# A new order of opening, batches and end in a fused attention and expert kernel, with dummy products, two output transfers and one tiny product

## Chip, cores and metric

The kernel runs on one core of one Trainium2 chip. The metric is the time of one execution on the device in microseconds (us), which is the median over the runs shown. Engines are named as in the profile: PE is TensorE (matrix products), PEld its weight loads, DVE is VectorE, ACT is ScalarE, SP the engine whose queue issues nearly all transfers.

## What is computed

Eight batches of eight heads: 512 rows of `x` and 32 rows of `state`, 64 wide, attend to each other; the result goes through a two-layer network with the Mish activation, all in float32.

```python
scores = softmax(x @ state.T / 8);  xread = scores @ state        # [8, 8, 512, 64]
scores2 = softmax(state @ x.T / 8); sread = scores2 @ x           # [8, 8, 32, 64]
x = concat([xread, sread], axis=2) -> (8 * 544, 512)
h = x @ w_in                       # w_in  512 x 2048
g = h * tanh(log1p(exp(h)))        # Mish
out = g @ w_out                    # w_out 2048 x 512
```

## The kernel before

The read of the state is folded into the first layer: `a @ (state @ w_in)`, so a batch needs `sw = state @ w_in` (small products of tiles of 64 by 32, `sw_product`) and then 128 x 128 x 256 products of the attention weights with it (`gemm1`, letter P). A large product is done with two-part operands (a rounded high part and the rest), three products for one. The hidden width is worked through in 8 slots of 256 columns.

For batches 0 and 1 the second layer is plain (`gemm2_wide`, letter g, 12 products). From batch 2 on it is done by a seven-product scheme on halves (`sums`, `high`, `low`, then `gemm2`): step U issues 12 products into two accumulator banks, step V 9 into two others, and P issues 12. So one slot of a unit (half a batch) is 33 large products. After 8 slots `combine` adds the four banks into the output tile `o` and sends it. A last unit "s" does the rows of the state for all batches; its output goes out in eight transfers of 32 rows.

Order is written out by hand. Every engine but POOL issues strictly in the order of the program (class `InOrder`): `OPENING` lists steps up to the first slots of batch 2, and then a loop over `periods` runs P two slots ahead of U and V, with the side work of the next batch put at fixed slots by the tables `STEADY`, `LAST` and `END`. The letters that matter:

- `SC` scores of a batch (32 small products), `RE` the read of `x` (64), `SW`/`SX` the products `state @ w_in`: `SW_j` in the opening is 16 small products in batch 0 and 32 later, `SX_0` and `SX_4` are 64 each and cover slots 0 to 3 and 4 to 7 of the next batch. `sw_four` issues SX in two halves, into two kinds of PSUM bank; `xh`, `xl` are the two-part split of its result on ACT and DVE.
- `in_e` (`stream`) brings slot e of `w_in` back from DRAM (512 KB). There are four places only: slots 0, 1, 4, 5 share the tiles `wi6` and `wi7`, slots 2, 3, 6, 7 the tile `x`. So `in_4` to `in_7` can be issued only after SX_0 has read slots 0 to 3. `LX` (transposed `x` of a batch) uses `wi6` and `wi7` too, `LN` (`x` itself) uses the tile `x`.
- In the opening: `lx` loads the two halves of batch 0's transposed `x`, `li` and `Lo` the raw weights, `hi`, `ci`, `ji`, `ho`, `co`, `jo` turn them into float32 on ACT and DVE, `sca` to `pil` are batch 0's attention, `pq` its first-layer products, `fill` and `warm` products of the identity whose result nobody reads.

In every batch the loop runs, on PE, SX_0 after slot 11's first part, SX_4 after slot 14's, and in slot 2 of the next batch RE and, one part later, SC. Between SX_0 and SX_4 lie 99 large products, between SX_4 and RE 132, between RE and SC 9, and from SC to the next SX_0 288.

Of the kernel before, what the change touches and what calls it, by code (L numbers as in the profile page):

```python
# [63 lines left out]
def state_attention_mish_kernel(ctx, tc, xT, xn, st, wiw, wow, out):  # L64
# [705 lines left out]
    run(OPENING, a=0, b=1, c=2, d=3)  # L770

    for n, (u, s) in enumerate(periods):
        if n < SLOTS:
            continue
        b, h = u
        now = SLOTS * h + s
        table = END if b == "s" else LAST if b == B - 1 else STEADY
        extra = {k: [v] for k, v in table.get(now, {}).items()}

        def beside(place):  # L780
            who = {} if b == "s" else dict(a=b, b=b + 1, c=b + 2)
            for text in extra.get(place, ()):
                run(text, **who)

        one, two = n + 1 < len(periods), n + 2 < len(periods)
        if two:
            gemm1(n + 2)
        beside("a0")
        if one:
            high(n + 1)  # L790
        beside("v0")
        if one:
            low(n + 1)
        beside("a1")
        if two:
            mish(n + 2)
        gemm2(n, 0)
        beside("pe")
        gemm2(n, 1)
        beside("pe2")  # L800
        beside("v1")
        if two:
            sums(n + 2)
        beside("a2")
        if s == SLOTS - 1:
            combine(u)
        beside("v2")
# [3 lines left out]
    lb tab lx_0 sca_0 sma_0 sma_1 lx_1 li_0 fill_1 tur_0 sca_1 top_0 sma_2 li_1 sma_3 li_2 lev_0 tur_1 Lo_0  # L811
    top_1 ev_0 tot_0 gua_0 rec_0 ci_0 hi_0 lev_1 ev_1 hi_1 warm nor_0 bac_0 ji_0 a.SW_0 pih_0 tot_1 gua_1 pil_0
    rec_1 a.wh_0 a.wl_0 hi_2 nor_1 di_2 pq_0 Lo_1 bac_1 ci_1 ji_1 ho_0 a.SW_1 js_0 li_5 li_3 pih_1 co_0 pil_1
    fill_2 fill_2 ji_2 a.wh_1 mh_0 a.wl_1 jo_0 pq_1 mh_1 a.SW_2 ho_1 a.wh_2 wo_0 gi_1 ci_5 lo_0 gj_1 gi_0 a.wl_2
    p_1 hi_3 ci_3 gj_0 ma_1 do_1 mb_1 ji_3 gh_1 g_3 g_2 jo_1 Lo_6 g_1 g_0 gl_1 a.SW_3 a.wh_3 a.wl_3 p_2 b.LX
    Lo_2 ma_2 mb_2 wo_1 lo_1 Lo_4 ho_2 p_3 hi_5 Lo_3 co_3 li_4 hi_4 g_10 do_2 gh_2 jo_2 g_13 g_12 wo_2 lo_2 gl_2
    ci_4 ji_4 ho_4 g_11 ho_3 jo_3 wo_3 ji_5 g_20 Lo_5 ho_5 li_6 g_23 a.SW_4 a.wh_4 co_5 a.wl_4 lo_3 mb_3 g_22
    g_21 ma_3 a.SW_5 p_4 js_2 co_4 gh_3 gl_3 jo_4 b.LS hi_6 ci_6 a.t2 a.wh_5 ma_4 mb_4 gh_4 a.wl_5 g_32 li_7
    wo_4 g_30 g_33 ji_6 p_5 Lo_7 gl_4 lo_4 a.x2_1 a.SW_6 a.wh_6 a.wl_6 js_5 g_31 g_41 g_42 a.x2_0 jo_5 co_6 ho_6
    g_43 ma_5 mb_5 ci_7 a.TU wo_5 lo_5 js_3 a.s2 g_40 js_6 hi_7 b.SC p_6 b.sc_1 gh_5 gl_5 b.sc_0 ji_7 g_53  # L820
    a.SW_7 mb_6 ma_6 jo_6 wo_6 b.tu b.to a.wh_7 a.wl_7 gh_6 g_50 b.le g_51 ho_7 b.x1 lo_6 b.SW_0 gl_6 p_7 js_4
    g_52 g_61 ma_7 b.wh_0 mb_7 b.ts b.no js_1 b.ba g_60 co_7 a.BU b.ph_0 a.LN b.ph_1 b.wl_0 g_62 g_63 b.pl_0
    a.RE b.LN b.pl_1 p_8 gh_7 gl_7 a.ro js_7 jo_7 wo_7 ma_8 mb_8 b.SW_2 p_9 lo_7 g_70 g_71 g_72 b.wh_2 b.wl_2
    gh_8 gl_8 mb_9 g_73 o_0 ma_9 p_10 gh_9 gl_9 mb_10 b.t2 o_1 b.SW_6 ma_10 b.wh_6 p_11 g_83 g_93 gh_10 b.wl_6
    o_2 o_3 g_81 g_91 b.SW_4 gl_10 b.x2_1 g_80 b.x2_0 c.LX ma_11 b.TU qs_0 b.wh_4 b.wl_4 g_101 qs_1 c.LS c.SC
    g_82 kh_0 kl_0 mb_11 qh_0 gh_11 gl_11 g_92 p_12 c.sc_0 ql_0 d.LS g_90 in_1 c.sc_1 in_0 c.SW_0 mb_12 qs_6
    g_102 c.wh_0 c.tu g_103 c.to kh_1 ma_12 g_113 g_100 c.le g_110 c.x1 g_112 g_111 in_5 c.t2 gh_12 gl_12 c.x2_0
    b.s2 c.wl_0 qh_1 c.ts p_13 g_121 ql_1 ma_13 c.no kl_1 mb_13 gh_13 qs_7 g_122 c.x2_1 qh_7 p_14 b.BU b.RE in_4
    gl_13 g_123 qh_6 c.ba in_2 ql_6 c.ph_0 ql_7 c.pl_0 g_133 ma_14 g_131 g_132 g_120 mb_14 b.ro qs_4 qh_4 ql_4
    in_3 c.SW_2 gh_14 g_130 c.wh_2 gl_14 c.wl_2 p_15 g_140 qs_5 ma_15 P_0 qh_5 c.SW_4 g_141 qs_3 g_142 ql_5  # L830
    mb_15 gh_15 kh_3 gl_15 qh_3 g_150 g_143 c.TU M_0 g_151 S_0 in_6 c.wh_4 in_7 kl_3 H_0 o_4 ql_3 P_1 o_5 g_152
    g_153 c.wl_4 M_1 L_0 S_1 o_6 c.ph_1 H_1 L_1 o_7 P_2 U_0 V_0 P_3 M_2 d.LX kh_7 S_2 qs_2 V_1 P_4 H_2 kh_2 kl_2
    qh_2 L_2 kh_4 kl_4 ql_2 kl_7 M_3 c.pl_1 M_4 U_1 S_3 c.SW_6 c.BU c.wh_6 kh_5 c.wl_6 c.s2 U_2 P_5 H_3 V_2 L_3
    c.LN S_4 M_5 kl_5 S_5 H_4 L_4 d.SC P_6 V_3 V_4 kh_6 kl_6 U_3 in_0 d.sc_0 M_6 S_6 d.sc_1 c.RE H_5 U_4 d.tu
    c.ro H_6 d.to P_7 L_5 U_5 L_6 V_5 M_7 S_7 H_7 d.le P_8 M_8 L_7 V_6 U_6 S_8 H_8 d.t2 L_8 P_9 in_2 U_7 M_9 S_9
    V_7 in_3 C_0 in_1
# [3 lines left out]
STEADY = {  # L840
    2: dict(pe="a.RE", pe2="b.SC", v1="a.ro", a2="b.sc_0 b.sc_1", v2="in_0 in_1 in_2 in_3"),
    3: dict(v0="b.tu"),
    4: dict(v0="b.to"),
    5: dict(v0="b.le"),
    6: dict(v0="b.t2"),
    8: dict(a2="b.x1 b.x2_0 b.x2_1"),
    9: dict(v0="b.ts b.s2", v2="b.no"),
    10: dict(v2="b.ba"),
    11: dict(pe="b.SX_0", a2="b.xh_0", v2="b.xl_0 in_4 in_5 in_6 in_7"),
    12: dict(a2="b.ph_0 b.ph_1", v2="b.pl_0 b.pl_1"),  # L850
    13: dict(v2="b.TU b.BU"),
    14: dict(pe="b.SX_4", a2="b.xh_4", v2="b.xl_4 b.LN c.LX c.LS"),
}
LAST = {
    0: dict(v2="in_0 in_1"),
    2: dict(pe="a.RE", v1="a.ro", v2="in_2 in_3"),
    7: dict(pe="ST", a2="sh", v2="sl"),
    12: dict(a2="WH_0", v2="WL_0 in_4"),
    13: dict(a2="WH_1", v2="WL_1 in_5"),
    14: dict(a2="WH_2", v2="WL_2"),  # L860
    15: dict(a2="WH_3", v2="WL_3 in_6 in_7"),
}
END = {
    0: dict(a2="WH_4", v2="WL_4"),
    1: dict(a2="WH_5", v2="WL_5"),
    2: dict(a2="WH_6", v2="WL_6"),
    3: dict(a2="WH_7", v2="WL_7"),
}
# [28 lines left out]
```

## Time and profile before

| | us |
|---|---|
| median of three runs | 634.57 |
| lowest and highest run | 631.49, 635.59 |
| the profiled execution | 632.25 |
| its span, first to last instruction | 630.5 |
| busy in the span: PE / DVE / ACT | 609.2 / 478.3 / 339.3 |

The profile is of one execution. Matmuls overlap on PE, so a PE that is busy throughout can still run at different pitches; how far apart equal groups of products start tells the pitch. In the chain of work (the view that follows the last instruction back to what released it) a row gives start, length, engine, what is written and how many instructions.

### The profile page before, as it was taken

The page shows a single profiled execution, that of the slowest core. Times are in us where ns is not written, and L with a number is a line of the kernel's source. Part 1 is how long each engine was busy: PE and PEld are TensorE (multiplying, and loading weights), DVE is VectorE, ACT ScalarE, POOL GpSimd, SP SyncE. Part 2 cuts the span into 40 slices and gives each one's busy share as a digit, 9 for nine tenths or more (in the row PEclk, how much of TensorE's full clock was granted, in tenths as well). Part 3 has the DMA queues.
Part 4 walks back from the last instruction along what each step waited for, and adds up shares of the span by engine and source line. Part 5 has one row for each costly group of instructions (what it writes and reads, how often), then busy time and mean ns, then how long its engine had stood idle before and what let it go on. Part 6 is the DMA issues. An engine that isn't in the chain of part 4 may idle for free.

```text
span 630.5 us, 15205 instructions
## 1 busy us (share of the span) xinstructions
PE 609.2 (97%) x6548; PEld 582.9 (92%) x6548; DVE 478.3 (76%) x874; ACT 339.3 (54%) x497; POOL 0.7 (0%) x6
## 2 busy tenths in 40 slices
PE   4899999899999999999999999999999999999995
PEld 3798899899999999999999999999999999999995
DVE  4786896589788888588868797679858886577753
ACT  4988763456355564347634754456534663445541
POOL 0000000000000000000000000000000000000000
PEclk9899999999999999999999999999999999999998
DMA  8976443642175234601563047403551165101201
GB/s 334 411 306 269 126 150 111 171 165 68 20 217 199 68 131 145 200 40 45 158 210 134 35 137 233 142 35 114 164 191 45 40 169 202 61 35 68 102 1 33
DMA packets 57267, 86.43 MB, mean 137 GB/s; under 512 B 35825, under 2 KB 38897, under 8 KB 54001
## 3 DMA queue, kind: packets, MB, share of 16 engines
q1 hardware_dynamic: 57056, 85.34, 40.2%
q8 instruction: 51, 0.84, 0.5%
q14 instruction: 16, 0.12, 0.1%
q10 hardware_dynamic: 144, 0.13, 0.1%
HBM read 68.16 MB, written 17.30 MB: 136 GB/s over the span
## 4 chain that ended last, share of the span: by engine, by line
PE 90%; ACT 4%; DVE 2%; DMA 2%; issue 1%; SPq 1%; DVEq 0%; ACTq 0%
PE ph_u L56 25%; PE acc L56 11%; PE ph L56 6%; PE swp L56 4%; PE sc L56 2%; PE srp L56 1%; ACT L56 1%; PE acc_(5, 1)_2_5548 L56 1%; PE acc_(6, 1)_2_6474 L56 1%; PE acc_(4, 1)_2_4622 L56 1%; PE acc_(3, 1)_2_3696 L56 1%; PE acc_(2, 1)_2_2770 L56 1%; PE acc_(2, 0)_0_2269 L56 1%; PE acc_(6, 0)_2_6044 L56 1%; PE acc_(4, 0)_2_4192 L56 1%
## 5 line engine op out<-in xcount | busy, mean ns | idle before, releaser
L56 ACT CAST Sh<-G 128x896 fp32r<-128x896 f32 x104 | 98.2, 944 | 134.7 <-DVE G L56 48.7
L56 PE MATMUL ph_u<-aT,sw 128*128 128x256 f32 x1152 | 150.2, 280 | 0.0
L56 DVE TENSOR_TENSOR Sl<-G,Sh 128x896 fp32r<-128x896 f32 x104 | 112.9, 1086 | 44.7 <-ACT Sh L56 44.2
L56 PEld LDWEIGHTS ph_u<-aT,sw 128*128 128x128 f32 x1152 | 141.0, 189 | 2.1 <-issue 2.1
L56 DVE TENSOR_TENSOR G<-G 128x128 f32<-128x128 f32 (+1 forms) x312 | 104.7, 335 | 22.0 <-ACT G L56 14.2
L56 PE MATMUL acc<-wo,gh 128*128 128x256 f32 x512 | 90.1, 280 | 0.0
L56 ACT ACTIVATE G<-ph_u 128x512 f32<-128x512 f32 x104 | 62.2, 599 | 49.3 <-PE ph_u L56 45.9
L56 PEld LDWEIGHTS acc<-wo,gh 128*128 128x128 f32 x512 | 77.4, 188 | 3.4 <-issue 3.3
L56 PE MATMUL acc<-wo,gl 128*128 128x256 f32 x256 | 71.1, 278 | 0.0
L56 PEld LDWEIGHTS ph<-aT,sw 128*128 128x128 f32 x384 | 47.0, 193 | 8.4 <-ACT turned L56 5.0
L56 PE MATMUL ph<-aT,sw 128*128 128x256 f32 x384 | 50.3, 287 | 4.0 <-ACT turned L56 2.5
L56 ACT CAST sw<-swp 128x512 fp32r<-128x512 f32 (+1 forms) x72 | 34.3, 549 | 29.4 <-PE swp L56 29.4
L56 PEld LDWEIGHTS acc<-wo,gl 128*128 128x128 f32 x256 | 48.4, 189 | 0.0
L56 DVE TENSOR_TENSOR sw<-swp,sw 128x512 fp32r<-128x512 f32 (+1 forms) x72 | 41.0, 623 | 9.5 <-ACT sw L56 9.5
L56 ACT ACT_TABLE_LOAD x29 | 37.2, 1283 | 8.2 <-PE ph L56 5.7
L56 PE MATMUL swp<-wi,bd 64*32 64x256 f32 x1024 | 33.8, 381 | 0.6 <-DVE wi L56 0.5
L56 ACT ACTIVATE turned<-ph 128x512 f32<-128x512 f32 (+1 forms) x34 | 18.5, 574 | 20.8 <-PE ph L56 16.1
L56 DVE STREAM_TRANSPOSE e<-sc 128x512 f32<-128x512 f32 x30 | 19.5, 688 | 9.5 <-ACT sc L56 9.3
L56 PEld LDWEIGHTS swp<-wi,bd 64*32 64x32 f32 x1024 | 18.4, 106 | 7.1 <-PE at L56 1.0
L56 DVE CAST gh<-turned 128x1024 fp32r<-128x1024 f32 (+1 forms) x17 | 11.2, 660 | 16.3 <-ACT turned L56 9.2
L56 PE MATMUL ph_u<-srT,whl 128*128 128x256 f32 x192 | 23.1, 276 | 0.0
L56 PEld LDWEIGHTS ph_u<-srT,whl 128*128 128x128 f32 x192 | 22.4, 188 | 0.0
(446 smaller groups left out, 1205.4 us busy)
## 6 DMA issues: line engine op xcount, KB each, us to landing
wi<-w_dram SPq DMA_DIRECT2D x56, 512.0 KB, 5.0
wir<-in_wi_dram SPq DMA_DIRECT2D x8, 1024.0 KB, 9.3
wor<-in_wo_dram SPq DMA_DIRECT2D x8, 1024.0 KB, 12.4
xn<-in_xn_dram SPq DMA_DIRECT2D x8, 1024.0 KB, 6.5
out_dram<-o SPq DMA_DIRECT2D x32, 256.0 KB, 3.2
xT<-in_xT_dram SPq DMA_DIRECT2D x14, 512.0 KB, 7.8
w_dram<-wi SPq DMA_DIRECT2D x8, 512.0 KB, 6.2
e_dram<-e SPq DMA_DIRECT2D x32, 128.0 KB, 3.0
```

The lines of the kernel that those rows point to most:

```text
L56: made = method(*args, **kwargs)
```

## The change

- `OPENING` is in a new order. Batch 0's two halves are taken in the other order; half 1 subtracts its maximum on PE (`les`) and takes the exponential from PSUM. 19 dummy steps are added and `warm_up` grows from 5 to 14 products; all dummies multiply a tile of zeros, set by DVE, in place of the identity.
- The first `x` comes as its own input, laid out so that each half is one contiguous block of 4 KB to a partition, where it was gathered in pieces of 512 bytes. The other batches' layout is unchanged.
- One step `nudge`: a product of 64 by 32 with 64 columns into a `misc` bank that nobody reads, after the products g_3 of the first slot and ahead of the scores of batch 1.
- The loop over `periods` with its tables is replaced by two texts of steps, `STEADY` for each of the batches 2 to 6 and `CLOSING`. In STEADY large products stand in another order (two P together, V ahead of U), and SX_0, SX_4, SC and RE move: counted in large products there are now 45 between SX_0 and SX_4, 174 from there to SC, 9 from SC to RE, 300 from RE to the next SX_0. The last batch has no SC behind it.
- `sw_four` does the half of slots j+2, j+3 first.
- `PRODUCTS`: block b22 goes from bank 2 to bank 3, so that `combine` adds bank 3 in one pass of 512 columns where there were two of 256.
- The last unit's output goes out in two transfers of 256 KB, one on SP's queue and one on ACT's, where there were eight on SP's.

```diff
-WARM = 5
+WARM = 14
+    zero = pool.tile([P, P], F32, name="zero")
+    nc.vector.memset(zero, 0.0)
...
-        sp.dma_start(t, xT[0][:, :, :, cols(h)])
+        sp.dma_start(t, x0T[h])
...
-                pe.matmul(pt[:, :P], ident, ident, start=True, stop=True)
+                pe.matmul(pt[:, :P], zero, zero, start=True, stop=True)
...
-                (2, 1, 6, "b22"), (3, 0, 1, "q4")]
+                (3, 0, 6, "b22"), (3, 1, 1, "q4")]
...
-        dve.tensor_add(c12, c12, m3)
-        dve.tensor_add(c21, c21, m4)
+        inner = o.rearrange("p r e -> p (r e)")[:, HALF:3 * HALF]
+        dve.tensor_add(inner, inner, acc(u, 3))
...
-                for b4 in range(4):
-                    r0 = (4 * (1 - r) + b4) * T + S
-                    sp.dma_start(out[r0:r0 + NS, :], o[cols(b4, NS), r])
+                to = out.rearrange("(b t) e -> b t e", t=T)[4 * (1 - r):4 * (2 - r), S:]
+                (act if r else sp).dma_start(to, o[:, r])
...
-        for i, bank in ((j, first_bank), (j + 2, misc)):
+        for i, bank in ((j + 2, misc), (j, first_bank)):
...
+    def nudge(i):
+
+        pt = misc(f"nudge_{i}")
+        pe.matmul(pt[:NS, :D], zero[:D, :NS], zero[:D, :D], start=True, stop=True)
...
 OPENING = """
...
+    a.SW_2 li_3 p_1 jo_0 wo_0 gj_1 a.wh_2 Lo_2 lo_0 g_3 nudge_0 Lo_3 gj_0 mb_1 ma_1 a.wl_2 do_1 ho_2 b.SC a.x2_1 co_3
...
+    g_91 qs_1 b.s2 g_102 ma_12 qs_0 mb_12 kh_1 kl_1 g_101 qh_0 c.LX c.SC qh_1 g_103 c.sc_1 g_113 p_13 c.sc_0
...
+STEADY = """
...
+    S_12 H_11 L_11 V_10 b.no H_12 P_14 L_12 P_13 M_13 V_11 U_11 S_13 M_14 U_12 b.SX_0 V_12 H_13 b.xh_0 S_14 b.ba
+    b.ph_0 b.ph_1 L_13 U_13 in_4 b.xl_0 in_6 P_15 H_14 b.pl_0 M_15 in_7 in_5 L_14 P_16 S_15 b.TU M_16 b.SX_4
+    U_14 c.LX V_13 V_14 b.xh_4 b.xl_4 P_17 b.pl_1 P_18 H_15 L_15 V_15 S_16 U_15 M_17 H_16 P_20 S_17 L_16 C_1
+    M_18 S_18 V_16 U_16 H_17 b.LN L_17 P_19 V_17 H_18 L_18 M_20 U_17 b.BU M_19 S_19 H_19 P_21 V_18 U_18 c.SC
+    L_19 V_19 c.sc_1 c.sc_0 S_20 in_0 H_20 b.RE in_3 c.tu M_21 in_2 c.t2 L_20 P_23 P_22 S_21 U_19 M_22 S_22 U_20
...
```

## Rows read from the trace of the kernel before

**Rows 1.** The page, busy time of the engines: us, share of the span, instructions.
```profile
PE 609.2 (97%) x6548; PEld 582.9 (92%) x6548; DVE 478.3 (76%) x874; ACT 339.3 (54%) x497; POOL 0.7 (0%) x6
```

**Rows 2.** By stage: length; busy PE, PEld, DVE, ACT, POOL; clock; DMA share, GB/s.
```profile
15.00:20.00 5.00, 4.42 (x36) 3.76 (x33) 3.93 (x9) 4.61 (x7) 0.00 (x0) 0.66 0.99 373
...
437.10:440.84 3.74, 3.74 (x35) 3.74 (x35) 3.67 (x8) 2.58 (x6) 0.00 (x0) 1.00 0.86 292
454.35:458.24 3.89, 3.89 (x35) 3.89 (x34) 3.68 (x10) 1.46 (x2) 0.00 (x0) 1.00 0.99 353
```

**Rows 3.** Waits of PE over the whole span: us in total, times, longest.
```profile
PE sc L56 <- DMA xT<-in_xT_dram: 5.2, 1, 5.2
PE ph L56 <- ACT turned L56: 2.5, 3, 2.1
PE sc L56 <- DMA bd<-in_st_dram: 1.8, 1, 1.8
```

**Rows 4.** Chain of work in two steady batches: start, us, what, instructions.
```profile
433.91 1.93 PE swp L56 x64
...
437.08 1.36 PE ph_u L56 x12
...
440.82 1.36 PE ph_u L56 x12
...
447.28 1.89 PE swp L56 x64
...
450.42 1.41 PE ph_u L56 x12
...
454.31 1.41 PE ph_u L56 x12
...
467.16 1.02 PE sc L56 x32
...
535.54 1.36 PE ph_u L56 x12
```

**Rows 5.** Chain of work in the opening, behind the scores of batch 2.
```profile
123.86 1.10 PE sc L56 x32
...
127.88 2.72 PE ph L56 x24
...
143.07 2.83 PE ph L56 x24
```

**Rows 6.** Transfers that write `wi` from 262 to 275 us: issues, then landing times.
```profile
L56 SPq DMA_DIRECT2D wi<-w_dram x4: 327/413/424, 262.7 to 264.1; - x4
...
DMA to landing us min/median/max: 3.2/5.4/7.1
```

**Rows 7.** The same for `xT` of batch 2, from 110 to 125 us.
```profile
L56 SPq DMA_DIRECT2D xT<-in_xT_dram x2: 383/392/401, 114.4 to 114.9; - x2
...
DMA to landing us min/median/max: 4.3/4.7/5.1
```

**Rows 8.** Last output: its eight issues in the timeline, landing of one (DMA view).
```profile
624.65 3.64 SPq L56 DMA_DIRECT2D out_dram<-o_s  x8
...
out_dram<-o_s SPq DMA_DIRECT2D x8, 64.0 KB, 1.7
```

**Rows 9.** Two output transfers of 256 KB near 590 us: issues, then landing times.
```profile
L56 SPq DMA_DIRECT2D out_dram<-o x2: 337/380/424, 590.0 to 590.4; - x2
...
DMA to landing us min/median/max: 2.2/2.7/3.1
```

**Rows 10.** Timeline: the first Mish on ACT, DVE passes of a steady batch.
```profile
22.73 0.66 ACT L56 ACTIVATE turned<-ph 128x256 f32<-128x256 f32 x2
...
361.81 1.09 DVE L56 TENSOR_TENSOR Sl<-G,Sh 128x896 fp32r<-128x896 f32 x1
...
363.81 1.30 DVE L56 STREAM_TRANSPOSE at<-e 128x512 f32<-128x512 f32 x2
...
367.28 2.48 DVE L56 TENSOR_TENSOR sw<-swp,sw 128x512 fp32r<-128x512 f32 x4 [0.21 <-ACT sw L56]
```

More of the change, by code (lines that the diff above doesn't have):

```diff
@@ L63, in state_attention_mish_kernel @@
 @with_exitstack
-def state_attention_mish_kernel(ctx, tc, xT, xn, st, wiw, wow, out):
+def state_attention_mish_kernel(ctx, tc, x0T, xT, xn, st, wiw, wow, out):
     nc = tc.nc
@@ L107, in load_xT @@
             for i in range(2):
-                sp.dma_start(xTs[b][i], xT[b][:, i])
+                sp.dma_start(xTs[b][i], xT[b - 1][:, i])
             return
@@ L111, in load_xT @@
         xTs[b] = [t[:, i] for i in range(2)]
-        sp.dma_start(t, xT[b])
+        sp.dma_start(t, xT[b - 1])
     def load_xn(b, tag="x"):
@@ L491, in stream @@
         else:
-            if e % 2 == 0:
-                streams["x"] = pool.tile([P, 2, NC, 2 * P], F32, tag="x", name=f"wi_{e}")
-            t = streams["x"][:, e % 2]
+            x = streams.pop(e ^ 1, None)
+            if x is None:
+                x = streams[e] = pool.tile([P, 2, NC, 2 * P], F32, tag="x", name=f"wi_{e}")
+            t = x[:, e % 2]
         w_in[e] = t
@@ L631, in combine @@
     def combine(u):
-        (m1, m2), (m6, m7), (m5, m3), (m4, _) = ((a[:, :HALF], a[:, HALF:]) for a in (acc(u, t) for t in range(4)))
+        (m1, m2), (m6, m7), (m5, _) = ((a[:, :HALF], a[:, HALF:]) for a in (acc(u, t) for t in range(3)))
         o = pool.tile([P, 2, DM], F32, tag="o", name=f"o_{u[0]}_{u[1]}")
@@ L694, in warm_up @@
         for _ in range(WARM):
-            pe.matmul(warm[:, :P], ident, ident, start=True, stop=True)
+            pe.matmul(warm[:, :P], zero, zero, start=True, stop=True)
     pw = {}
@@ L740, in state_attention_mish_kernel @@
         "o": lambda i: out_wide(*divmod(i, 4)),
-        "fill": lambda n: a0.fill(n, acc(0, 3)), "qs": q_sums, "qh": q_high, "ql": q_low, "kh": q7_high, "kl": q7_low, "in": stream,
+        "nudge": lambda i: nudge(i), "fill": lambda n: a0.fill(n, acc(0, 3)), "qs": q_sums, "qh": q_high, "ql": q_low, "kh": q7_high, "kl": q7_low, "in": stream,
         "WH": ws_high, "WL": ws_low,
@@ L750, in state_attention_mish_kernel, with run @@
     }
-    def run(text, **batch):
+    def run(text, first, letters):
+        batch = {who: first + i for i, who in enumerate(letters)}
+        n0 = 2 * SLOTS * max(0, first - FIRST)
         for step in text.split():
@@ L763, in run @@
             elif what in ("U", "V"):
-                gemm2(i, what == "V")
+                gemm2(n0 + i, what == "V")
             elif what == "C":
-                combine(units[i])
+                combine(units[n0 // SLOTS + i])
+            elif what in "PMSHL":
+                common[what](n0 + i)
             else:
                 common[what](i)
[L770 to L807, printed above, removed]
@@ L810 @@
-OPENING = """
[L811 to L836, printed above, removed]
@@ L837 @@
-"""
[L840 to L868, printed above, removed]
+    run(OPENING, 0, "abcd")
+    for b in range(FIRST, B - 1):
+        run(STEADY, b, "abc")
@@ new lines @@
+"""
+STEADY = """
+    H_9 P_10 c.LS L_9 V_8 P_11 U_8 V_9 M_10 S_10 b.x1 b.x2_0 b.ts H_10 L_10 P_12 b.x2_1 M_11 S_11 U_9 U_10 M_12
+    S_12 H_11 L_11 V_10 b.no H_12 P_14 L_12 P_13 M_13 V_11 U_11 S_13 M_14 U_12 b.SX_0 V_12 H_13 b.xh_0 S_14 b.ba
[3 more added lines that the diff above has]
+    L_19 V_19 c.sc_1 c.sc_0 S_20 in_0 H_20 b.RE in_3 c.tu M_21 in_2 c.t2 L_20 P_23 P_22 S_21 U_19 M_22 S_22 U_20
+    V_20 H_21 L_21 V_21 U_21 c.to M_23 b.s2 S_23 H_22 L_22 H_23 L_23 P_24 M_24 S_24 V_22 c.le U_22 b.ro P_25
+    H_24 in_1 L_24 M_25 S_25 V_23 U_23 C_2
@@ new lines @@
+"""
+CLOSING = """
+    P_10 H_9 L_9 M_10 U_8 ST V_8 S_10 sh sl P_11 H_10 L_10 M_11 U_9 V_9 S_11 P_12 H_11 L_11 M_12 U_10 V_10 S_12
+    P_13 H_12 L_12 M_13 U_11 V_11 S_13 P_14 H_13 L_13 M_14 U_12 V_12 S_14 WH_0 WL_0 in_4 P_15 H_14 L_14 M_15
+    U_13 V_13 S_15 WH_1 WL_1 in_5 P_16 H_15 L_15 M_16 U_14 V_14 S_16 WH_2 WL_2 P_17 H_16 L_16 M_17 U_15 V_15
+    S_17 WH_3 C_1 WL_3 in_6 in_7 P_18 H_17 L_17 M_18 U_16 V_16 S_18 WH_4 WL_4 P_19 H_18 L_18 M_19 U_17 V_17 S_19
+    WH_5 WL_5 P_20 H_19 L_19 M_20 U_18 V_18 S_20 WH_6 WL_6 P_21 H_20 L_20 M_21 U_19 V_19 S_21 WH_7 WL_7 P_22
+    H_21 L_21 M_22 U_20 V_20 S_22 P_23 H_22 L_22 M_23 U_21 V_21 S_23 H_23 L_23 U_22 V_22 U_23 V_23 C_2
@@ L871 @@
+"""
 def kernel(**inputs):
@@ L879 @@
     turned = state.reshape(B, NC, 2, NS, D).transpose(0, 4, 2, 1, 3).reshape(B, D, 2, NC * NS)
+    xT = x6.transpose(0, 5, 6, 2, 1, 4, 3).reshape(B, P, 2, NC, HALF)
     arrays = {
-        "in_xT_dram": x6.transpose(0, 5, 6, 2, 1, 4, 3).reshape(B, P, 2, NC, HALF),
+        "in_x0T_dram": xT[0].reshape(P, 2, NC, 2, P).transpose(3, 0, 1, 2, 4),
+        "in_xT_dram": xT[1:],
         "in_xn_dram": x.reshape(B, NC, 2, P, NT, D).transpose(0, 3, 1, 2, 4, 5),
```

26 lines of the change are left out of this document (added).

## The prediction, made before the changed kernel was run

> **What bounds the kernel now.** I read the page first, then the stages, the waits of PE and the chain of work. PE is busy for 609 of 630.5 us, DVE for three quarters of the span [rows 1], and in the steady batches it is busy without a gap (3.74 of 3.74 us, 3.89 of 3.89) [rows 2]. So behind the opening an edit of DVE, ACT or SP can gain nothing by itself; it can only lose time, by making PE wait. PE's waits lie ahead of that: 5.2 us for the first `x`, 2.5 us for the first Mish, 1.8 us at the scores of batch 2 for a transfer [rows 3]. Behind the last product comes an end of some 6 us for the output [rows 8].
>
> A busy PE is not at one pitch, and that is the second thing the reader is to see. One slot is 33 large products. The two slots behind SX_0 start 3.74 us apart, the two behind SX_4 3.89 us [rows 4]: 113.3 ns a product and 117.9 ns, 4.5 ns more, though the granted clock is 1.00 in both [rows 2]. Twelve products take 1.36 us at the one pitch, 1.41 us at the other. The pitch holds for as long as large products follow each other and changes at a block of 32 or 64 small ones: fast behind SX_0, slow behind SX_4, and behind the RE of the last batch, which has no SC after it, fast (1.36 us) up to the end [rows 4]. RE and SC, 9 products apart, change it twice. I read this as a toggle: SX_0, SX_4, RE and SC each flip the pitch, so of a batch's 528 products 132 + 288 = 420 are slow, which costs 420 x 4.5 ns = 1.9 us. A block that PE had to wait in is another matter: the SC of batch 2 waited 1.8 us for its transfer [rows 3], and the products behind it came at the fast pitch (24 in 2.72 us), a later stretch at the slow one (24 in 2.83 us) [rows 5].
>
> **The change part by part**, against the profiled execution's 632.25 us.
>
> *End, -1.7 us.* Eight issues take 3.64 us from 624.65, the last of them starts about 0.45 us before their end and lands 1.7 us later [rows 8]: 624.65 + 3.64 - 0.45 + 1.7 = 629.5. Two transfers of 256 KB landed 2.2 and 3.1 us after their own issues, which were 0.4 us apart [rows 9], so 3.5 us after the first. Issued on two queues I take 3.1 us: 627.8, which is 1.7 us less; bounds -1.3 (3.5 us) and -2.5 (both in 2.2 us). The single pass of 512 columns in place of two of 256 lies in the last microsecond of DVE and I take it as nothing; it is one of eight passes, so at most 0.3 us either way. The Trainium skill (DMA: Bandwidth & Descriptors, Issuing engines are not separate DMA queues) says that transfers from two engines run on the same 16 engines and save only the issue time. By it the pair gains no more than the 0.4 us that I took off.
>
> *Opening up to batch 0's first products, -1.0 us.* PE waits 5.2 us for the first half of `x` [rows 3]. The new layout brings it in longer pieces; no row shows such a load at the start, so 0 is one bound, and the other is the time from issue to landing that two later 512 KB loads of `x` took, 4.3 to 5.1 us [rows 7], which would be no gain. In between, I take 1.0 us earlier, as less queueing of the raw weights behind it. From there to the first Mish at 22.73 us [rows 10] ACT is a queue of passes over the raw weights, and the new order puts one more ahead of it, so the lead does not grow. The dummies cost nothing while PE waits anyway; they should remove the stretch at 15 to 20 us with a mean clock of 0.66, part of it at the lower level of 1.2 GHz [rows 2], which lies ahead of that same wait for Mish and so is worth 0 here. Bounds for the part: +1.0 and -2.5.
>
> *Pauses up to 110 us, -1.0 us.* Of the 2.5 us waited for Mish [rows 3] some 2.1 us are the first one; the rest, and like pauses that fall in the opening, can be filled by other products: batch 1's scores and the g steps now stand ahead. I take 1.0 us, bounds 0 and -2.
>
> *The tiny product, 0.* It waits for a `misc` bank that DVE's `wl_2` gives back. Right behind it stands SC of batch 1, which needs both `misc` banks, so that wait is there without it. Its own price is at most that of a block of 32 such products, 1.02 us [rows 4]; two instructions, so I take 0. What it may do is to flip the pitch.
>
> *Loads in the opening, 0.* `c.LX` now stands behind `in_0` and `in_1`, whose tiles it takes over, so it can be issued only when `c.SW_0` has read them. Until `c.SC` PE has 36 products, 4.1 us, and the load's halves, issued 0.5 us apart, land 4.3 and 5.1 us after their issues [rows 7], the second so 5.6 us after the first issue: a wait of up to 1.4 us in place of the 1.8 us of before. `c.SW_2` behind RE is short of its slots by a few tenths in the same way. Sum 0; bounds -1.5 and +2.
>
> *The reload between SX_0 and SX_4, +6.2 us.* Here I expect the loss. `in_4` is the first of four loads on SP's queue, and its tile is read until three quarters of SX_0 are done, since slots 2 and 3 now go first. Count from the start of SX_0, which takes 1.93 us [rows 4]: `in_4` goes out at 1.45. Four such loads issued over 1.4 us landed 3.2 us (the first) to 1.4 + 7.1 = 8.5 us (the last) after the first issue [rows 6], nearly evenly, so `in_7`, third, at 1.45 + 6.7 = 8.2 and `in_5`, last, at 9.95. PE gets to SX_4 at 1.93 + 45 products (5.2) + 0.1 = 7.2. Its quarters of 0.47 us need slots 6, 7, 4, 5: slot 7 at 7.7 waits to 8.2, then slot 5 at 9.2 waits to 9.95. That is 1.25 us a batch, five batches, 6.2 us. Before, 99 products (11.3 us) stood there and covered it. Bounds: 0.3 and 1.7 us a batch (the last landing 1 us sooner, or 0.45 us later), 1.5 to 8.5 us. The Trainium skill (DMA: Bandwidth & Descriptors, Anatomy of one DMA) fits a transfer as 2.0 us plus bytes over 436 GB/s, which as an estimate lands the fourth 6.8 us after the first issue. By it nothing waits and this term is 0; the row, 8.5 us, speaks against it.
>
> *Pitch, -2.1 us.* With a wait inside every SX_4 the pitch behind it starts anew; rows show one such case fast [rows 5], and I take even chances. Half of 528 products slow in place of 420 is 156 x 4.5 ns = 0.7 us less, times five: -3.5. The products behind the last RE, 774 before and all fast, are now 648 and half slow: 324 x 4.5 ns = +1.4. Bounds: fast behind every SX_4 leaves 54 slow a batch (45 and 9) and a slow end, -366 x 4.5 ns x 5 + 648 x 4.5 ns = -8.2 + 2.9 = -5.3; slow behind every one gives +54 x 4.5 ns x 5 = +1.2 and a fast end.
>
> Sum: 632.25 - 1.7 - 1.0 - 1.0 + 0 + 6.2 - 2.1 = 632.6. The profiled execution lies 2.3 us below the median of 634.57, within what the runs differ by, so I leave it there: 632.5.
>
> **The rivals.** *A, the loads come in time and the pitch turns fast.* Nothing waits in SX_4, the toggle holds through all batches, and each has 54 slow products in place of 420. 632.25 - 3.7 - 5.3 = 623.2. For it: the loads would be in time if they landed 2 us sooner than in rows 6; the first lands after 3.2 us. Against it: all that rows 6 shows, and that the pitch must also fall right, at which the tiny product may help or harm. Its side of the 2.0 us fit is the skill's rule above.
>
> *B, in time but the pitch stays slow.* 632.25 - 3.7 + 1.2 = 629.8.
>
> *C, DVE is late between SX_0 and the U behind SX_4.* There DVE has two high-low subtractions (1.09 each), two sums (taken as long), two pairs of transposes (1.30 a pair), four parts of `sw` (2.48) and one part of the attention weights (taken as half a pair, 0.65) [rows 10]: 10.1 us. PE gives it SX_0, 45 products and SX_4, 9.0 us. P behind SX_0 needs banks that DVE empties. If DVE comes to SX_0 2 us late, PE waits about 3 us a batch; below 1.25 us it hides in the reload's wait, and from there it decides. 632.25 - 3.7 + 15 - 2.1 = 641.5, slower. For it: more work than time. Against: DVE is idle a quarter of the span.
>
> *D, nothing is gained in the opening* because transfers of raw weights pace it: 632.5 + 2 = 634.5.
>
> **How the numbers follow.** My case 0.50, A 0.20, B 0.12, C 0.13, D 0.05. With the bounds above my case alone runs from 626 to 638. The range for all reaches to A and most of C: 623 to 640. About 1% of the median, 6.3 us, is what a measurement here tells from no change: below 628.2 or above 640.9. Faster: 0.09 of my case, 0.18 of A, 0.03 of B, 0.01 of the rest, 0.31. Slower: 0.05 of my case, 0.09 of C, 0.02 of the rest, 0.16. The rest is 0.53.
>
> **What would show it.** Right: PE waits on a DMA of `wi` in the middle of SX_4 in each steady batch, for about 1.2 us; the pitch behind these waits differs from batch to batch; the last two output transfers land some 3.1 us after their issue. Wrong: no wait at SX_4, and slots 3.74 us long almost throughout (A) or 3.89 us (B); waits of P or U for DVE (C). The step I trust least is the landing of the four loads: if they land in 6.5 us, 6 us of my sum are gone.

## The result and the profile after

The changed kernel takes 639.0 us (median of 20 runs, 633.90 to 646.14) where the kernel before takes 634.56 (20 runs beside it): a ratio of 1.0056, interval 1.0036 to 1.0077. Runs more than 1.5% above the fastest of the same kernel, two of these 20, are left out of a ratio, so that it is smaller here than the quotient of the two medians. The changed kernel is slower by half a per cent, where 632.5 was forecast. That lies in the range, and within the 1% of "no change", but the interval excludes a gain, and the parts of the sum, below, did not all come as forecast. The profiled execution takes 638.64 us with a span of 636.8 (before 632.25 and 630.5), so it is 6.39 us longer, and this is what the steps have to explain. It is more than the 3.6 us of the ratio, in part because the profiled execution of before lies 2.3 us below its median.

The page of after, busy PE, answers [rows 1]; beneath it a stage of the opening (length; busy PE, PEld, DVE, ACT, POOL; clock; DMA share and GB/s), which answers the first of [rows 2].

```profile
PE 616.7 (97%) x6620; PEld 585.6 (92%) x6620; DVE 477.4 (75%) x859; ACT 337.0 (53%) x497; POOL 0.7 (0%) x6
```
```profile
15.00:20.00 5.00, 4.97 (x60) 4.26 (x53) 4.71 (x10) 4.89 (x9) 0.00 (x0) 1.00 1.01 421
```

The dummies fill PE and the clock of that stretch is now 1.00 where it was 0.66. The waits of PE over the whole span (us in total, times, longest), against [rows 3]:

```profile
PE swp L56 <- DMA wi<-w_dram: 5.1, 7, 1.4
PE ph L56 <- ACT turned L56: 1.6, 1, 1.6
PE acc L56 <- DVE zero L92: 1.1, 1, 1.1
PE sc L56 <- ACT sc L56: 0.5, 1, 0.5
PE sc L56 <- DMA xT<-in_xT_dram: 0.4, 1, 0.4
```

The wait for the first `x` is gone from the list, since dummies stand there, the scores of batch 2 wait 0.4 us where they waited 1.8, and one wait is new: the first layer's small products for the weights brought back, `wi`. The chain of work through SX_0, SX_4 and SC of one steady batch (start, us, what, instructions) shows it on the path, and answers [rows 4]:

```profile
438.44 0.71 PE acc_(5, 1)_1_5596 L56 x6
439.14 1.54 PE swp L56 x48
441.15 0.35 SPq L56
441.55 0.43 SPq L56
442.38 7.13 DMA wi<-w_dram
449.56 0.67 PE swp L56 x16
450.22 0.89 PE acc_(5, 1)_0_5589 L56 x6
...
458.93 1.36 PE ph_u L56 x12
...
469.47 0.68 PE acc_(6, 0)_1_6083 L56 x6
470.15 1.02 PE sc L56 x32
...
471.73 0.71 PE acc_(6, 0)_3_6069 L56 x6
```

PE gets through 48 of SX_0's 64 products, then the chain leaves PE for SP's queue and the fourth load, and comes back 7.13 us later for the last 16 products of SX_4. It also shows the two pitches: six large products take 0.71 us ahead of SX_0, 0.68 behind SX_4, and 0.71 again behind SC. The same place in the timeline of PE, with the idle time ahead in brackets, and the loads (issues, then landing), which answer [rows 6]:

```profile
446.27 0.66 PE L56 MATMUL swp<-wi,bd 64*32 64x256 f32 x16
448.33 1.89 PE L56 MATMUL swp<-wi,bd 64*32 64x256 f32 x48 [1.40 <-DMA wi<-w_dram]
```
```profile
L56 SPq DMA_DIRECT2D wi<-w_dram x4: 320/339/433, 440.7 to 442.4; - x4
...
DMA to landing us min/median/max: 3.5/5.5/7.1
```

The end, in the timeline, against [rows 8]; and by stage behind it:

```profile
626.81 0.69 DVE L56 TENSOR_TENSOR o_s<-o_s,acc_('s', 0)_3_7825 128x512 f32<-128x512 f32 x1
627.53 0.69 SPq L56 DMA_DIRECT2D out_dram<-o_s  x1
627.53 1.40 ACTq L56 DMA_DIRECT2D out_dram<-o_s  x1
```
```profile
630.00:632.00 2.00, 0.00 (x0) 0.00 (x0) 0.00 (x0) 0.00 (x0) 0.00 (x0) 0.50 0.22 70
632.00:634.00 2.00, 0.00 (x0) 0.00 (x0) 0.00 (x0) 0.00 (x0) 0.00 (x0) 0.50 0.26 101
634.00:636.00 2.00, 0.00 (x0) 0.00 (x0) 0.00 (x0) 0.00 (x0) 0.00 (x0) 0.50 0.20 76
```

Both are issued at 627.53, and the span ends at 636.8, 9.3 us later. The columns to read are the last two: a share of at most 0.26 of the 16 DMA engines is at work, and 101 GB/s is all that moves, with nothing else in flight. From the start of the last large product (625.44) to the span's end it is 11.40 us, where it was 7.44 before.

### The profile page after: what moved, and what is told of

Its sections match the earlier page's. It is cut to its first block, busy times and chain, and to the rows that moved or that the text cites. A ratio compares the mean times of both kernels' runs of the same rounds, so it can differ in the third digit from the quotient of the medians.

```text
span 636.8 us, 15345 instructions
## 1 busy us (share of the span) xinstructions
PE 616.7 (97%) x6620; PEld 585.6 (92%) x6620; DVE 477.4 (75%) x859; ACT 337.0 (53%) x497; POOL 0.7 (0%) x6
## 4 chain that ended last, share of the span: by engine, by line
PE 87%; DMA 8%; ACT 1%; SPq 1%; DVE 0%; issue 0%; DVEq 0%
PE ph_u L56 22%; PE acc L56 13%; PE ph L56 7%; DMA wi<-w_dram 5%; PE swp L56 4%; DMA wor<-in_wo_dram 2%; PE srp L56 1%; PE sc L56 1%; PE acc_(2, 0)_0_2392 L56 1%; PE acc_(5, 0)_0_5152 L56 1%; PE acc_(4, 0)_0_4228 L56 1%; PE acc_(3, 0)_0_3304 L56 1%; PE acc_(5, 0)_1_5159 L56 1%; PE acc_(4, 0)_1_4235 L56 1%; PE acc_(3, 0)_1_3311 L56 1%; PE acc_(5, 0)_3_5145 L56 1%
## 5 line engine op out<-in xcount | busy, mean ns | idle before, releaser
L56 PE MATMUL ph_u<-aT,sw 128*128 128x256 f32 x1152 | 146.0, 279 | 0.0
L56 PEld LDWEIGHTS ph_u<-aT,sw 128*128 128x128 f32 x1152 | 138.7, 188 | 0.9 <-issue 0.4
L56 ACT ACTIVATE G<-ph_u 128x512 f32<-128x512 f32 x104 | 60.6, 598 | 83.0 <-PE ph_u L56 59.5
L56 PEld LDWEIGHTS ph<-aT,sw 128*128 128x128 f32 x384 | 45.5, 188 | 5.1 <-ACT turned L56 2.6
L56 PE MATMUL ph<-aT,sw 128*128 128x256 f32 x384 | 48.1, 281 | 1.6 <-ACT turned L56 1.6
L56 PE MATMUL swp<-wi,bd 64*32 64x256 f32 x1024 | 36.0, 383 | 5.5 <-DMA wi<-w_dram 5.1
L56 PEld LDWEIGHTS swp<-wi,bd 64*32 64x32 f32 x1024 | 15.4, 105 | 16.9 <-DMA wi<-w_dram 10.8
L56 DVE TENSOR_TENSOR gl<-turned,gh 128x1024 fp32r<-128x1024 f32 (+1 forms) x17 | 19.7, 1159 | 2.5 <-ACT gh L56 1.9
```

The source lines that it names most:

```text
L56: made = method(*args, **kwargs)
```

## The experiments

Each ratio is to the kernel before, run beside it on the same chip; a difference of two ratios times 634 us gives the difference of two kernels, which is clear of the noise only where the intervals lie apart.

**The end.** Theory: the two transfers are slow by themselves. First each kernel gets the other's end.

after with before's end (`end_eight`):
```diff
-(act if r else sp).dma_start(to, o[:, r])
+for b4 in range(4):
+    r0 = (4 * (1 - r) + b4) * T + S
+    sp.dma_start(out[r0:r0 + NS, :], o[cols(b4, NS), r])
```


> The changed kernel with the last output sent in eight transfers on SP's queue again, all else as changed. Theory (the end is what failed in the sum): from the start of the last output's issues to the end of the span the changed kernel takes 9.3 us and the one before 5.8 us, so this run ends some 3.5 us earlier than the changed kernel, at about 635.5 us, and is the same as before within 0.3%. Rival (the end is only a shift, and the reload waits of 7.8 us carry the loss): it stays within 1 us of the changed kernel's 639.

before with after's end (`before_two`):
```diff
-for b4 in range(4):
-    r0 = (4 * (1 - r) + b4) * T + S
-    sp.dma_start(out[r0:r0 + NS, :], o[cols(b4, NS), r])
+to = out.rearrange("(b t) e -> b t e", t=T)[4 * (1 - r):4 * (2 - r), S:]
+(act if r else sp).dma_start(to, o[:, r])
```


> The kernel before with the last output sent in two transfers, one on SP's and one on ACT's queue, nothing else changed. Theory: the two transfers by themselves cost 3.5 us, so about 638 us, slower by 0.5%, and the DMA view of the last 12 us shows about 100 GB/s in place of up to 220. Rival (the price comes from the new order around it): 633 us, as I forecast for this term.

Measured: 637.28 us, ratio 1.0034 (1.0002 to 1.0067), so 1.4 us less than after by the medians' ratios; its profiled execution is 635.23, 3.4 less. The intervals of the two overlap, so the totals alone do not show it. `before_two` takes 638.52 us, ratio 1.0051 (1.0026 to 1.0077), so the end alone makes the kernel before 3.2 us slower. The traces show both: from the last product to the span's end it is 7.84 us in `end_eight`, where after has 11.40, and 11.16 in `before_two`, where before has 7.44. Each end takes its time along, whatever stands ahead of it.

Then, is it the two queues, the size, or the shape? The eight small transfers on two queues, behind after (`end_split`) and behind before (`before_split`), and after's in four of 128 KB with an outermost dimension of 2 (`end_pairs`):

```diff
 for b4 in range(4):
     r0 = (4 * (1 - r) + b4) * T + S
-    sp.dma_start(out[r0:r0 + NS, :], o[cols(b4, NS), r])
+    (act if r else sp).dma_start(out[r0:r0 + NS, :], o[cols(b4, NS), r])
```


> After with the last output in eight transfers of 64 KB, four on SP's queue and four on ACT's, in place of two of 256 KB. Theory (each of the two large transfers runs over 4 of the 16 DMA engines; small ones run over all, and two queues halve the time of the issues): from the start of the last product to the span's end 11.4 us become about 6, so the time falls by about 5 us against after, to about 634, and 1 to 2 us under the kernel with eight transfers on SP's queue alone. Rival (the end is long because two queues get in each other's way): no more than 1 us under after.

> The kernel before, with four of its last eight output transfers issued on ACT's queue in place of SP's. Theory (eight issues one behind the other are half of what lies behind the last product; the transfers themselves run over all DMA engines): 1.0 us less than before, as between the kernels with this end and the one with eight on SP's queue behind the new batches, 7.8 to 6.5 us from the last product to the end. Rival (two queues slow each other, which would make the loss of after's end one of the queues and not of the shape of the transfers): the same as before or longer.


```diff
-(act if r else sp).dma_start(to, o[:, r])
+for b4 in (0, 2):
+    (act if r else sp).dma_start(to[b4:b4 + 2], o[b4 * NS:(b4 + 2) * NS, r])
```


> After with the last output in four transfers of 128 KB, two on each queue, the outermost dimension of each 2 instead of 4. Theory (as many DMA engines work at a transfer as its destination's outermost dimension has steps, which is why 4 of 16 worked in after): 2 engines a transfer, 64 packets of 2 KB each, 5.4 us a transfer at 84 ns a packet; if the four land on the same two engines, some 22 us from the last product's start to the span's end or more (11.4 in after), if they land on different ones, about 9. Rival (a transfer is slow because it is large, or because two queues carry it): between after's 11.4 and the 6.5 us of eight transfers, thus about 8 to 9 us, with all engines or most of them at each transfer.

Measured: `end_split` 633.05 us, 0.9993 (0.9971 to 1.0015), 4.0 us less than after by the ratios; 6.46 us from last product to end. `before_split` 633.85, 1.0002 (0.9977 to 1.0028): its end is 1.3 us shorter in the profile (6.11 us), but what lies ahead differs more from run to run than that, and the total shows no gain. `end_pairs` (two runs) 645.06, 1.0178 (1.0136 to 1.0221), 7.7 us more than after, with 16.7 us from last product to end. By stage, behind the issues, first `end_split`, then `end_pairs` (last columns: DMA share, GB/s):

```profile
628.00:630.00 2.00, 0.00 (x0) 0.00 (x0) 0.00 (x0) 0.00 (x0) 0.00 (x0) 0.94 0.77 216
```
```profile
634.00:636.00 2.00, 0.00 (x0) 0.00 (x0) 0.00 (x0) 0.00 (x0) 0.00 (x0) 0.50 0.13 51
636.00:638.00 2.00, 0.00 (x0) 0.00 (x0) 0.00 (x0) 0.00 (x0) 0.00 (x0) 0.50 0.13 51
```

An outermost dimension of 4 has 0.26 of the 16 engines at work and 101 GB/s, one of 2 has 0.13 and 51 GB/s, and transfers of 32 rows have 0.77 and 216. Half the dimension halves the share and the rate, though there are more and smaller transfers; so it is neither the size nor the two queues. Shares of 0.26 and 0.13 are 4 and 2 engines, as many as the dimension has steps, although two and four transfers are in flight: all of them use the same few engines. The expected 22 us were too many because I counted the packets of a transfer of 64 rows at each of its two engines in place of half of them: 512 KB at 51 GB/s are 10.3 us, at 101 they are 5.2, and 11.4 + 5.1 = 16.5.

The Trainium skill states this (DMA: Bandwidth & Descriptors, Rules for kernel authors, *Use all 16 engines*): the number of engines follows from the slowest dimension of both access patterns that is larger than one, and an outermost dimension below 16 confines the transfer to at most that many. The runs agree at 4 and at 2. It is the rule that I should have held against the change.

**The reload.** after, without the loads `in_4` to `in_7` of the steady batches; SX_4 there reads slots 0 to 3 instead, so this kernel leaves out part of the weights' traffic and multiplies by others.

```diff
+if skip[0] and e >= 4:
+    w_in[e] = w_in[e - 4]
+    return
```


> The changed kernel without the loads of slots 4 to 7 in the five steady batches: SX_4 reads the slots 0 to 3 that are still there, so that part of the first layer is left out and the rest of the work is the same. Theory: the five waits in SX_4, 7.8 us in the profile, go, and with no wait left the pitch toggles at each block in the same way in every batch, 54 slow products a batch and a slow end, some 900 in place of 1980 behind the first SX_0, which is 4.8 us more: about 626.5 us, with slots 3.74 us long behind RE in every steady batch. Rival (the waits go but the pitch is not settled by the blocks): 631 us and batches of either pitch.

Measured: 630.14 us, 0.9929 (0.9908 to 0.995), 8.1 us less than after by the ratios. Every SX_4 takes 1.58 us from its first product to its last, where after's take 2.38, 2.86, 3.82, 3.58 and 2.14; with what PE waits ahead of the first of them, after loses 7.8 us to the reload in five batches. As expected, the pitch then turns at each block, alike in all five batches. From the start of the first SX_0 to the last large product the profile has 386.7 us where that of after has 397.6, so 10.9 us less: 7.8 are the waits and 3.1 the pitch, by some 700 slow products fewer.

The time is 3.6 us short of the gain expected, and the profile shows two reasons. I had put 1,980 slow products behind the first SX_0 of after; its trace has 1,704, so the pitch could not give the 4.8 us that I took. And the profiled execution comes to its first SX_0 at 231.72 us, after at 227.86, though the steps up to there are the same. Of these 3.9 us 2.0 are lost by 27.4 us: PE waits 2.1 us for the first Mish, and from 25 to 27 us the granted clock is 0.50, the lower of its two levels, 1.2 GHz. `old_order` waits as long there at a clock of 1.00 throughout, so what brings the lower level is not shown.

**The tiny product.** after without `nudge`:

```diff
-    a.SW_2 li_3 p_1 jo_0 wo_0 gj_1 a.wh_2 Lo_2 lo_0 g_3 nudge_0 Lo_3 gj_0
+    a.SW_2 li_3 p_1 jo_0 wo_0 gj_1 a.wh_2 Lo_2 lo_0 g_3 Lo_3 gj_0
```


> The changed kernel without the tiny product. Theory (it turns what the block of batch 1's scores does to the pitch): the 96 large products behind these scores, at 31 us, come at 117.8 ns in place of 113.3, and the pitch of all blocks up to the scores of batch 2, which wait for a transfer, is the other way round; in time that is worth about +0.6 us against the 0.35 us that the tiny product takes: 639 us, no difference. Rival (it does nothing to the pitch): 638.7 us and the products at 31 us still 113.3 ns apart.

Measured: 640.66 us (four runs), 1.0113 (1.0065 to 1.0162), 3.6 us more than after, though the intervals overlap a little. The chains about batch 1's scores, first after, then without the tiny product:

```profile
25.45 2.93 PE ph L56 x24
28.39 1.36 PE acc L56 x12
29.75 0.23 PE nudge L56 x2
29.97 1.15 PE sc L56 x32
31.12 2.93 PE ph L56 x24
34.05 6.01 PE acc L56 x53
```
```profile
25.51 2.93 PE ph L56 x24
28.45 1.36 PE acc L56 x12
29.80 1.02 PE sc L56 x32
30.83 3.02 PE ph L56 x24
33.85 6.24 PE acc L56 x53
```

With it the block costs 0.36 us more, and the 53 products behind it take 6.01 us, 113.4 ns each, as those ahead; without it 6.24 us, 117.7 ns. So the tiny product keeps the fast pitch over the block. It keeps the slow one too: in all eleven profiles of kernels with it the pitch behind this block is the one ahead, in nine of them the fast one and in two (`end_eight` and `no_reload`) the slow one. How far that carries depends on the next waits, so that the 3.6 us are this pair's, not the product's price.

That suggests the same product ahead of every block. `tick` writes one, of zeros, into the block's own bank, and the block then overwrites it.

```diff
+def tick(ap):
+    if ticking[0]:
+        pe.matmul(ap[:NS, :D], zero[:D, :NS], zero[:D, :D], start=True, stop=True)
...
     self.pss = [misc(f"sc_{b}_{u}") for u in range(2)]
+    tick(self.pss[0])
```

RE, SW and SX get the same call.

In the kernel before, nothing else changed (`before_ticks`):

> The kernel before, from batch 1's SC on with one tiny product of zeros ahead of each block of 32 or 64 small products, in the block's own bank; nothing else is changed. Theory (a block turns the pitch and one tiny product undoes it): the pitch of the large products is fast at batch 1's SC, stays so to the wait at batch 2's SC at 124 us, and from there keeps whatever it falls to: if fast, some 9 us less than before, 625; if slow, some 7 us more, 641; in both cases without the change at each block. Rival (the tiny product does nothing to the pitch): the changes at the blocks stay, 633 to 635.

Measured: 632.29 us, 0.9967 (0.9941 to 0.9992). In the trace of before every one of the 33 blocks of 32 or 64 behind 70 us turns the pitch but one, in which PE waits 1.8 us. In this one the fast pitch goes over every block in which PE does not wait, and turns slow only at the scores of batch 2 (a wait of 1.3 us for `bd`) and in three of the five SX_0, in each of which PE now waits 0.46 us. A slow pitch comes out fast from RE or SW and stays slow over SX_4. The gain is only 2.1 us of the 9 that it could be. Behind 200 us of the profile the pitch gives back 5.9 us, but the blocks take 4.7 us more. PE comes fast into SX_0 and waits there, 0.46 us a batch; and the tiny products have a price that I had left out: RE with one takes 0.22 us longer, SC and each SX 0.07, in all 0.42 us a batch.

**The order of batches.** after's opening, before's loop with its 99 products between SX_0 and SX_4, the end as in `end_split` (`old_batches`):

```diff
-for b in range(FIRST, B - 1):
-    run(STEADY, b, "abc")
-run(CLOSING, B - 1, "a")
+for n, (u, s) in enumerate(periods):
...
```


> The opening of after with its tiny product, behind it the order of batches of before (99 products between SX_0 and SX_4), and the end in eight transfers on two queues. Theory (the loss of the new batches is the wait for the reload): no wait inside SX_4, so 7.8 us less than end_split from that alone, less or more by the pitch: if SC in the steady batches starts fast, 108 products of a batch are slow, else 420, a difference of 1.4 us a batch. Together 624 to 629. Rival (the waits at SX_4 only take the place of time that is lost elsewhere in any case, as in the pitch or at other waits): 631 to 634.

Measured: 632.54 us, 0.9976 (0.9954 to 0.9998), only 1.1 us less than `end_split`, with intervals that overlap. The waits for `wi` are gone, and the rival's others are there; waits of PE:

```profile
PE ph_u L56 <- DVE sw L56: 6.2, 10, 0.7
```

Twice a batch PE stops for `sw`, behind the nine products of the step V that follow SX_0 and SX_4 (the expectation below miscounts them as seven), 7.9 us in all by the starts of the products. The edit that fits is the swap in `sw_four`: P behind the block needs the first bank, which DVE now empties last. Undone (`old_order`):

```diff
-for i, bank in ((j + 2, misc), (j, first_bank)):
+for i, bank in ((j, first_bank), (j + 2, misc)):
```


> The kernel old_batches, with the order of the halves inside SX as in the kernel before (slots j and j+1 into the first bank first, then j+2 and j+3 into the misc banks). Theory (of the change it is this swap that makes the old order of batches wait twice a batch, 0.8 to 1.0 us behind the seventh product after SX_0 and after SX_4, since P needs the first bank and DVE now empties it last): the ten waits, 7.9 us in the profile, go: 632.5 - 7.9 = 624.6, 622 to 628 with the pitch. Rival (DVE has too much to do there in any order, and the waits only move): 630 to 633.

Measured: 628.11 us (four runs), 0.9902 (0.9865 to 0.9939), 4.7 us less than `old_batches`. No wait of PE between 200 and 560 us is left in the list. That the waits come from the order of the halves is shown; after itself does not have them, since its order has other products there. What came back of the 7.9 us is less because more products are slow, some 2,200 in place of 1,300: over 113.4 ns a product the pitch costs 9.5 us in the one profile and 5.7 in the other.

**Ticks on top.** `old_batches` with `tick` ahead of each block from 79 us on, and the same with three blocks of the opening a few products later, so that PE does not come to them before their loads (`no_waits_ticks`):

```diff
-    in_0 c.SW_0 c.wh_0 ql_7 b.BU c.wl_0 g_91 qs_1
+    in_0 g_91 c.SW_0 c.wh_0 ql_7 b.BU c.wl_0 qs_1
...
-    c.LX c.SC qh_1 g_103 c.sc_1 g_113 p_13 c.sc_0
+    c.LX qh_1 g_103 g_113 p_13 c.SC c.sc_1 c.sc_0
...
-    kh_0 c.SW_2 g_122
+    kh_0 g_122 c.SW_2
```


> The kernel old_batches, and from batch 1's SW_0 on one product of 32 columns of zeros ahead of every block of 32 or 64 small products, written into the block's own bank. Theory (such a block turns the pitch of the large products, and one tiny product undoes it): the pitch is the same before and behind every block, so it changes only where PE has waited; 113.3 ns nearly throughout gives 3 to 8 us less than old_batches, 117.8 ns nearly throughout gives up to 8 us more; either way the pairs stop changing at blocks. Rival (the pitch is set by something else, as what the banks or the other engines do): it changes at the same blocks as in old_batches.

> The kernel old_batches_ticks, with three blocks of the opening moved a few products later (SW_0 and SW_2 of the third batch behind one product each, its SC behind three), so that PE no longer waits for their loads. Theory (with the tiny products the pitch turns only at a wait of PE; at batch 1's SW_0 it was fast in each profile of this opening): 113.3 ns from about 80 us to the end, no wait behind 110 us, about 620 us. Rival (pitch falls slow at some other place): 625 to 632 us.

Measured: 632.74 us, 0.9982 (0.9962 to 1.0001), and 630.72 us, 0.9949 (0.9929 to 0.9969). The pitch does what the theory says, with one exception in each profile, a slow stretch that comes out fast from RE without a wait. The chain about RE and SC of batch 4 in `old_batches`, then with ticks:

```profile
326.49 1.03 PE srp L56 x64
...
328.07 0.69 PE acc_(4, 0)_3_4230 L56 x6
328.76 1.02 PE sc L56 x32
...
332.10 0.71 PE acc_(4, 0)_1_4219 L56 x6
```
```profile
327.72 1.25 PE srp L56 x66
...
329.52 0.69 PE acc_(4, 0)_3_4249 L56 x6
330.22 1.09 PE sc L56 x27
...
333.56 0.68 PE acc_(4, 0)_1_4238 L56 x6
```

The 288 products behind SC are slow in the one and fast in the other; behind the other three such SC they are fast in both. And the time hardly moves: a batch, from SX_0 to SX_0, takes 69.01 us in the mean in the one and 68.95 in the other. By the starts of PE's instructions the fast pitch gives back 4.7 us over the whole profile, and nearly all of it goes into the blocks, which take 4.5 us longer: the price of the ticks, and in the opening loads for which an earlier PE waits longer. The waits for `sw` stand in both and are only 0.3 us longer. Half of this theory held (the pitch), and the numbers of the other half fell (the time). In `no_waits_ticks` the 2 us come from the waits of the opening.

All that helped in one (`old_order_ticks`), and the same with SX_0 behind U and V instead of between them (`old_order_late`):

```diff
-11: dict(pe="b.SX_0", a2="b.xh_0", ...
+11: dict(pe2="b.SX_0", a2="b.xh_0", ...
```


> All that helped, in one: the opening of after without its waits at the third batch's loads, the old order of batches with the old order of halves in SX, a tiny product ahead of each block, eight output transfers on two queues. Theory: 630.7 less the ten waits of 8.3 us, 622.4, with 113.3 ns between the products from 80 us to the end. Rival (what is freed is lost again at other waits): 626 to 630.

> The kernel old_order_ticks, with SX_0 of the steady batches moved behind the products U and V that stood behind it. Theory (in the fast pitch PE comes to SX_0 0.46 us before the first bank is free; with a few more products ahead it does not wait, and the pitch is not turned to slow there): five waits and the slow 99 products behind each go, 2.3 us plus 99 x 4.45 ns x 5 = 2.2 us, 4.5 us less than old_order_ticks, 622. Rival (the wait moves to the next product that needs that bank): no less than 625.

Measured: 626.29 us, 0.9883 (0.985 to 0.9916), and 624.79 us, 0.9862 (0.9835 to 0.989). The last is the fastest of all, by the ratios 12.3 us or 1.9% less than after. Neither is clear of the noise against `old_order` (0.9865 to 0.9939), so what the tiny products are worth there in time is not shown. Both miss their numbers, by 4 and 3 us. In the first each SX_0 waits 0.46 us and the 99 products behind it are slow; in the second that is gone, but a wait for `sw` stands behind SX_0 instead:

```profile
227.03 0.89 PE L56 MATMUL swp<-wi,bd 64*32 64x256 f32 x22
228.56 1.64 PE L56 MATMUL ph_u<-aT,sw 128*128 128x256 f32 x12 [0.64 <-DVE sw L56]
```

So the rival's wait is there, smaller than what was won. A steady batch takes 68.39 us before, 69.94 after (mean of four), 66.74 without the reload, 68.40 in `old_order_ticks` and 67.67 in `old_order_late`.

## Why the prediction was right and wrong

| step | forecast, us | profile of after, us |
|---|---|---|
| end | -1.7 | +3.95 |
| opening up to the first products | -1.0 | 0.0 |
| pauses up to 110 us | -1.0 | -2.1, and +0.36 for the block with the tiny product |
| tiny product | 0 | in the 0.36 |
| loads in the opening | 0 | -1.1 |
| reload between SX_0 and SX_4 | +6.2 | +7.8 |
| pitch | -2.1 | -1.85 |
| the rest (changes between kinds of products) | - | -0.7 |
| sum | +0.4 | +6.4 |

**The end is the step that failed**, 5.65 of the 6 us by which the sum is off. I took the landing of two transfers of 256 KB from [rows 9]. Those have 128 rows in the outermost place; these have 4. The row was right for its shape and said nothing on this one. Bounds of -1.3 and -2.5 were both bounds of the wrong thing: I had none for a change of shape. The rule of the Trainium skill that I did weigh there (DMA: Bandwidth & Descriptors, *Issuing engines are not separate DMA queues*) was beside the point. The traces agree with it: eight transfers on two queues end 1.3 to 1.4 us sooner than on one (6.46 against 7.84 us, 6.11 against 7.44), less than half of the 3.64 us that eight issues take [rows 8]. Without this term the sum forecast 2.1 us more than before, and `end_eight`, which is after with before's end, takes 2.1 us more by its ratio (0.1 to 4.2).

**The reload** was right in kind, place and near in size. PE came to SX_4 7.2 us behind SX_0's start, as forecast (439.07 to 446.27), the first load went out 1.6 us behind it (forecast 1.45), the last landed 8.8 us behind that (forecast 8.5). Per batch PE loses 0.56 to 2.25 us, 1.56 in the mean, where 1.25 was forecast and 1.7 the upper bound. The estimate of 6.8 us that the prediction set against the row was 2.0 us short. The spread is the landing of the loads: the last one landed 5.8 to 7.3 us after its issue had ended in the four batches whose trace has it.

**The pitch** came out near the sum by luck. Of 4,576 distances between the starts of products 2,108 are slow where 2,512 were, which costs 9.36 us where it cost 11.2. But the parts are not those of the sum. From the first SX_0 to the last RE 0.5 us were won where 3.5 were forecast: behind four of the five SX_4 with a wait the pitch is slow, behind one fast, against the even chances that I took. Behind the last RE nothing changed where 1.4 us more were forecast, and 744 products stand there, not the 648 of the prediction. Some 1.3 us were won in the opening, where I had none.

Nor do the steps of the kernel settle the pitch. The profiles of after, `end_eight`, `end_split` and `end_pairs`, the same up to the output, have 1,704, 681, 1,101 and 261 slow products from the first SX_0 to the last RE, and 0, 744, 744 and 744 behind it. So each number of slow products here is that of one execution. That the tiny product holds the pitch at its block, which I had named as a possibility and priced at 0, is shown.

**The opening** brought nothing at its start: batch 0's first 24 products in a row stand at 25.38 us, before at 25.37. The chain there (start, us, what):

```profile
3.14 14.01 DMA wor<-in_wo_dram
...
18.80 1.08 ACT wor L56
...
21.50 1.28 ACT L56
22.79 0.39 ACT turned L56
```

The path is the raw weights' transfer and ACT's passes over them, and the first Mish stands at 22.79 us against 22.73 [rows 10]. From 5 to 20 us all DMA engines are busy (a share of 1.01 to 1.03 in each stage). So rival D's mechanism decided here, to which I gave 0.05. An earlier `x` could not help. Its first half landed only 0.2 us earlier (4.82 us against 5.03), and the first scores began later (5.62 against 5.16), behind dummies that wait 1.1 us for DVE's zeros. Behind it the pauses and the wait at batch 2's scores gave 3.2 us where I had allowed 1.0.

Rival C (DVE late behind the blocks) did not show in after. It does in `old_batches`, 7.9 us, by the one edit that I had costed nowhere on its own: the swap of the halves in `sw_four`. A and B needed the loads in time, and fell.

## What to carry to other kernels

Ahead of merging transfers look at the outermost dimension on both sides: two large transfers with 4 steps there ended 3.6 to 3.7 us later than eight small ones with 32 rows. A row of the trace prices a transfer only if its shape is the same. And where PE is busy throughout, taking products out from between a load's issue and its use is only free if the row of that load's landing says so; here the 45 products left cost 7.8 us. And what one profile shows of the pitch has to be seen in a second one of the same steps before it is put down to an edit.

## What had not been expected of the hardware

Large products of one form run at two pitches, 113.3 and 117.8 ns, at a granted clock of 1.00 in both. A block of 32 or 64 small products that PE gets through without a wait turns the one into the other (32 of the 33 blocks of the kernel before behind 70 us; in all sixteen profiles, behind 26 us, 303 of the 305 without a tick that took no longer than such a block does elsewhere, and 5 of the 14 that took 0.06 us longer or more). A block of 16 leaves the fast one fast (61 of 62), and one more tiny product ahead of the block keeps the fast one: in `old_order_late` it holds over all blocks from 80 to 540 us. There the last 609 products are slow, behind the eight transposes of the state (`ST`) at 546.9 us and without a wait of PE, which is 2.7 us still to be had; in twelve of the sixteen profiles these eight leave the pitch as it is. After a wait, too, either pitch can follow. On what that depends, and why there are two, stays open.
